# Attention outputs and output weights as float16 halves instead of fp32r halves

## The chip, the cores and the metric

The kernel runs on one core of one Trainium2 chip. The metric is the device time of one execution in microseconds. A profile of one execution lies beside the times; its engines are called PE (TensorE matmul), PEld (TensorE weight load), DVE (VectorE), ACT (ScalarE), POOL (GpSimd) and SP (SyncE, which issues the DMAs).

## The reference

A transformer block with adaptive layer norm: sliding-window attention over a cache, then a gated MLP. Cut to what matters:

```python
# x [1, 2048, 576]; k_cache, v_cache [1, 16, 2048, 128]; wq [576, 32*128]; wo [32*128, 576]
# w1, w3 [576, 4608]; w2 [4608, 576]; c [1, 576]; w_mod [576, 6*576]
sa, ca, ga, sb, cb, gb = split(silu(c) @ w_mod, 6)
h = layernorm(x) * (1 + ca) + sa
q = heads(h @ wq)                                   # 32 heads of 128
k, v = last 512 keys of the cache, each of 16 kv heads serving 2 query heads
p = softmax(q @ k.T * 128**-0.5)
x = x + ga * (concat_heads(p @ v) @ wo)
h = layernorm(x) * (1 + cb) + sb
out = x + gb * ((silu(h @ w1) * (h @ w3)) @ w2)     # everything in float32
```

## The kernel before

A float32 product is made from halves: each operand is split into a high part (the value rounded to a narrower type) and a low part (the rest), and three products are added: high times high, high times low, low times high. Most operands are split into two fp32r halves, which are 4 bytes each. The softmax weights `p` and the values `v` are already split into two float16 halves, scaled first so that float16 can hold them.

The 2048 rows are four blocks of 512. The attention phase walks 128 *slots*: first blocks 0 and 1 for all 32 heads (half 0), then blocks 2 and 3 for all heads (half 1). Mostly a head's two blocks are neighbouring slots, so in half 0 a new head begins at every even slot. Each slot has four *steps* (`t` = 0 to 3) of 128 query rows. The main loop (`for i in range(n + 2)`) writes the instructions of one step in a fixed order, and each engine runs its own in that order:

- the scores of this step (three products `pss`, then the row maximum `nm` on DVE), the transposes of an earlier step's `p` on PE (`turn_by_pe`, three steps behind), two to four products of the query projection for a later slot (`quad`);
- `weights`: the low half of an earlier transposed `p` (`turn`, on DVE), then the exponential on ACT;
- `attend_out`, nine steps behind: one head's output for 128 rows times the head's output weights. `back` makes six products of 128x288 (three pairs of halves, two halves of the 576 columns) into the PSUM tile `E`; DVE then multiplies `E` by `r`, one over the softmax sum, and adds it to the accumulator `acc`. There is one `E`, so the next step's `back` cannot begin before DVE has read it;
- `run(i, t)`: a table of side tasks put at fixed steps with `at(i, t, task, ...)`: loads, splits, and pieces that prepare the MLP's weights, which `lay` spreads over the steps by a table of POOL costs (`cost`).

At the end of a slot `values` makes `po`, the head's output, with twelve float16 products. ACT scales it into the high half `oth`, DVE makes the low half `otl`, and DVE takes the reciprocal `r`.

The output weights of a head (`wo`, 128x576) pass through half 0 once: `load_out` reads them, `gate` multiplies them by the gate on POOL, `split_out` writes the high half on ACT and the low half on POOL, and `store` writes both to DRAM (`kept`). In half 1 `reload` reads the halves back. `undo` undoes the per-row scale that `prepare_v` gave to `v`; before, ACT and DVE apply it as they read `po`.

After the attention phase (from about 1752 us in the profile) comes the MLP, which is PE work from end to end and does not use these functions.

Of the kernel before, what the change touches and what calls it, by code (L numbers as in the profile page):

```python
# [8 lines left out]
F32 = mybir.dt.float32  # L9
F32R = mybir.dt.float32r  # L10
F16 = mybir.dt.float16
AF = mybir.ActivationFunctionType
ALU = mybir.AluOpType
AX = mybir.AxisListType
# [3 lines left out]
P = 128  # L18
D = 576
# [3 lines left out]
SB = 512  # L23
NSB = S // SB
ST = SB // P
HQ, HKV, DH = 32, 16, 128
# [4 lines left out]
HALF = D // 2  # L31
# [11 lines left out]
ORDERED = {mybir.EngineType.PE, mybir.EngineType.DVE, mybir.EngineType.Activation, mybir.EngineType.Pool, mybir.EngineType.SP}  # L43
SCALE = float(DH) ** -0.5
LIFT = 2.0**14
BY_DMA = (0,)
AFTER_EXP = 3
SETTLE = 2
TINY = 1e-30
# [3 lines left out]
def tile_block(  # L53
# [16 lines left out]
    nc = tc.nc  # L70
    k0 = k_cache.shape[3] - W

    const = ctx.enter_context(tc.tile_pool(name="const", bufs=1))

    columns = ctx.enter_context(tc.tile_pool(name="columns", bufs=2))
# [20 lines left out]
    def half_split(a):  # L96
        return a.rearrange("p (a n) -> p a n", a=2)

    soon, then, running = [], [], []

    def do(jobs):
        due = jobs[:]
        jobs.clear()
        for job in due:
            job()
# [6 lines left out]
    def split_slowly(hi, lo, src, eng):  # L112

        if not running:
            return split(hi, lo, src, eng)
        nc.scalar.copy(hi, src)
        soon.append(lambda: eng.tensor_sub(lo, src, hi.bitcast(F32)))
# [108 lines left out]
    def norm_stats(b, t):  # L226
        if t == 0:
            norms[b] = odd.tile([P, ST, 2], F32, tag="mv", name="mv"), []
        st = odd.tile([P, 2, 6], F32, tag="bst", name="bst")
        for h in range(2):  # L230
            nc.vector.bn_stats(st[:, h, :], row(b, t)[:, h * HALF : (h + 1) * HALF])
        passing.pop((b, t), None)
        nc.vector.bn_aggr(norms[b][0][:, t, :], st.rearrange("p a b -> p (a b)"))
# [77 lines left out]
    kept = {}  # L311

    def store(h):
        kept[h] = dram.tile([P, 2, D], F32, name=f"kept{h}")
        for e, a in enumerate(wos[0, h]):
            nc.sync.dma_start(kept[h][:, e, :], a.bitcast(F32))

    def reload(h):
        o = pool.tile([P, 2, D], F32R, tag="o", name="o", bufs=3)
        nc.sync.dma_start(o.bitcast(F32), kept[h])  # L320
        return o[:, 0, :], o[:, 1, :]

    def load_in(w, lo):
# [14 lines left out]
        nc.sync.dma_start(raw, w[lo : lo + P, :])  # L338
        return raw

    def split_out(raw):
        o = pool.tile([P, 2, D], F32R, tag="o", name="o", bufs=3)
        split_slowly(o[:, 0, :], o[:, 1, :], raw, nc.gpsimd)
        return o[:, 0, :], o[:, 1, :]

    undo = const.tile([P, HKV], F32, name="undo")
    vkept = {}

    def turned_by_dma(out, pieces):
# [3 lines left out]
    def prepare_v(g, raw):  # L353

        vs = pool.tile([P, 2, W], F16, tag="kv", name="vs", bufs=8)
        u = columns.tile([P, 2], F32, tag="u", name="u", bufs=2)
        nc.vector.tensor_reduce(u[:, :1], raw, axis=AX.X, op=ALU.max, apply_absolute_value=True)
        nc.vector.tensor_scalar(u[:, :1], u[:, :1], TINY, 1.0 / LIFT, op0=ALU.max, op1=ALU.mult)
        nc.vector.reciprocal(u[:, 1:], u[:, :1])
        nc.vector.tensor_scalar(undo[:, g : g + 1], u[:, :1], 1.0 / LIFT, None, op0=ALU.mult)  # L360
        vals[0, g] = raw, u, vs

    def split_v(g):
# [159 lines left out]
    def values(i):  # L523
        half, h, b = slots[i]
        st = state[i]
        v, pt = vals[half, h // 2], st["pt"]
        po = bank("S", "po")
        steps = [(e, 0, j) for j in range(KC) for e in range(2)] + [(0, 1, j) for j in range(KC)]
        for k, (d, e, j) in enumerate(steps):
            nc.tensor.matmul(po, v[:, d, j, :], pt[:, e, j, :], start=k == 0, stop=k == 3 * KC - 1)  # L530
        oh = pool.tile([P, SB], F32R, tag="ah", name="oth", bufs=3)
        ol = pool.tile([P, SB], F32R, tag="al", name="otl", bufs=3)
        scale = undo[:, h // 2 : h // 2 + 1]
        nc.scalar.activation(oh, po, AF.Copy, scale=scale)  # L534
        nc.vector.scalar_tensor_tensor(ol, po, scale, oh.bitcast(F32), op0=ALU.mult, op1=ALU.subtract)  # L535
        r = columns.tile([P, ST], F32, tag="r", name="r", bufs=3)
        nc.vector.reciprocal(r, st["l"])
        st["o"], st["r"] = (oh, ol), r

    def attend_out(i, t):  # L540
# [478 lines left out]
    def at(i, t, task, *args):  # L1019

        tasks.setdefault((i, t), []).append((task, args))
# [33 lines left out]
    for key, i in first.items():  # L1055
        h, kv = key[1], (key[0], key[1] // 2)
        if 2 < i < 4 * PLAIN:
            at(i - 3, 1, load, wqs, key, load_in, wq1, h * DH)
            at(i - 2, 1, put, wqs, key, split_in)
        if key[0]:  # L1060
            at(i - 1, 0, load, wos, key, reload, h)
        elif i > 2:
            at(i - 2, 1, load, wos, key, load_out, wo, h * DH)
            at(*(i - 1, 0) if i > 6 else (i, 0), gate, wos, key, "a")
            at(*(i - 1, 2) if i > 6 else (i, 2), put, wos, key, split_out)
            at(i + 1, 0, store, h)
        if i > 2 and h % 2 == 0:
            at(i - 3, 0, load, keys, kv, load_k, h // 2)
            at(i - 2, 2, put, keys, kv, split_k)
            if key[0]:  # L1070
                at(i, 1, load, vals, kv, reload_v, h // 2)
            else:
                at(i - 2, 0, load_v, h // 2)
                put_v_at(4 * i - 3, h // 2)
                at(i + 1, 1, keep_v, h // 2)
# [7 lines left out]
    at(4, 1, keep_v, 1)  # L1083
    for h in range(3):
        at(*((0, 1), (1, 1), (2, 1))[h], load, wos, (0, h), load_out, wo, h * DH)
        at(*((1, 2), (2, 0), (3, 1))[h], gate, wos, (0, h), "a")
        at(*((1, 3), (2, 2), (3, 2))[h], put, wos, (0, h), split_out)
        at(3 + h, 0, store, h)

    last_group = len(groups) - 1  # L1090

# [72 lines left out]
    def lay(items, first, STEP):  # L1164

        spare = []

        def cost(task, args):
            if task is put:
                return {split_in: 1580, split_out: 1440}.get(args[2], 0)  # L1170
            return {gate: 1440, last_q: 1300, lower_v: 1300, norm_rows: 330, make_h: 1300}.get(task, 0)

        def pass_fixed(upto):
            while clock[0] < upto:
                fixed = sum(cost(*job) for job in tasks.get(divmod(clock[0], 4), ()))
                clock[1] = max(clock[1], clock[0] * STEP) + fixed
                clock[0] += 1

        clock = [first - 4, 0]
        step, ends = first, []  # L1180
        for number, (fill, pieces) in enumerate(items):
            begin = ends[number - 2] + 1 if number > 1 else first - LEAD + number
            at(*divmod(begin, 4), fill)
            step, when = max(step, begin + LEAD), []
            for (behind, ahead, after), jobs in pieces:
                if behind is not None:
                    step = max(step, when[behind] + 2)
                pass_fixed(step + 1)
                while clock[1] + ahead + after > (step + 1) * STEP + ROOM:
                    step += 1  # L1190
                    pass_fixed(step + 1)
                clock[1] += ahead + after
                when.append(step)
                work(step, *jobs)
            ends.append(step + 2)
        return step
# [264 lines left out]
    for i in range(n + 2):  # L1461
        run(i, -1)
        for t in range(ST):
            do(soon)
            if i <= n:
                halve(4 * i + t)
            if i == n:
                turn_by_pe(4 * i + t)
                turn(4 * i + t)
            if i < n:  # L1470
                made = scores(i, t)
                turn_by_pe(4 * i + t)
            if i + 1 < 4 * PLAIN:
                query(i + 1, t)
            for piece in qsteps.pop(4 * i + t, ()):
                quad(*piece)
            if i < n:
                weights(i, t, *made)
            do(then)
            if i >= m0:  # L1480
                for _ in range(3 if (i, t) == (n + 1, 0) else 1):
                    next(stream)
            for back_step in range(max(4 * i + t - 9, 0), 4 * i + t - 8 + ((i, t) == (n + 1, 3))):
                attend_out(*divmod(back_step, 4))
            run(i, t)
        if 1 <= i <= n:
            values(i - 1)
        if i == n:
            turning.close()
            after = ctx.enter_context(tc.tile_pool(name="after", bufs=1, space=PSUM))  # L1490
            lane[1] = (E, after.tile([P, 2, 512], F32, tag="T2", name="pf"))
# [65 lines left out]
```

## Time and profile before

| | |
|---|---|
| time, median of 3 runs | 2955.62 us (2955.44 to 2955.67) |
| profiled execution | 2954.41 us |
| its span in the profile | 2952.6 us |
| busy share of the span | PE 98%, PEld 81%, DVE 68%, ACT 53%, POOL 59% |
| granted TensorE clock | 0.998 |
| attention phase | up to about 1752 us, then the MLP |

The profiled execution is 1.2 us below the median, 0.04%. Products overlap in the PE's pipeline, so the duration of one product is longer than its share of the time; the distance from one start to the next is what a row of products costs. PEld shows weight loads, which run beside products.

### The profile page before, as it was taken

Reading aid. Unit: us, or ns where it says so; the run is one execution under the profiler, and the core shown is the slowest. Engines: PE = TensorE matmul, PEld = TensorE weight load, DVE = VectorE, ACT = ScalarE, POOL = GpSimd, SP = SyncE. Lnnn points to the kernel's source line nnn. Section 1 sums busy time; section 2 is a strip of 40 time slices with the busy share of each in tenths; the row PEclk is TensorE's granted clock in tenths of the full one; section 3 lists DMA queues with packets and bytes.
Section 4 is the critical chain, followed back from the end, with each engine's and each line's share of the span. In section 5 each row is a group of like instructions: output and inputs, shape, how many; then the busy total and the mean of one; then the engine's idle time right before and its main releaser. Section 6 shows DMA issues by size and latency. Waiting matters only on the chain.

```text
span 2952.6 us, 47355 instructions
## 1 busy us (share of the span) xinstructions
PE 2903.8 (98%) x16056; PEld 2384.8 (81%) x16056; DVE 2011.1 (68%) x3149; ACT 1560.9 (53%) x3251; POOL 1751.2 (59%) x1884
## 2 busy tenths in 40 slices
PE   7999999999999999999999999999999999999999
PEld 6777777777777777777777778888888888888887
DVE  7877787777777877777777766555555555555556
ACT  6667777777656776677677543333333222222322
POOL 3678888888712877777878223355564544334345
PEclk9999999999999999999999999999999999999999
DMA  6989999999885999989889946677766766666664
GB/s 216 280 266 347 277 345 311 298 289 299 260 277 179 326 301 295 296 284 283 273 278 299 300 154 202 218 233 251 251 226 202 286 231 199 205 198 193 202 201 143
DMA packets 441205, 751.27 MB, mean 254 GB/s; under 512 B 185730, under 2 KB 185730, under 8 KB 437380
## 3 DMA queue, kind: packets, MB, share of 16 engines
q1 hardware_dynamic: 440964, 748.25, 79.1%
q8 instruction: 128, 2.10, 0.3%
q14 instruction: 113, 0.93, 0.1%
HBM read 474.97 MB, written 235.37 MB: 241 GB/s over the span
## 4 chain that ended last, share of the span: by engine, by line
PE 80%; DVE 7%; ACT 4%; issue 2%; POOL 1%; DMA 1%; SPq 0%; ACTq 0%; POOLq 0%; DVEq 0%
PE py L797 15%; PE px L797 11%; PE po L530 10%; PE pe L428 10%; PE pf L910 7%; PE pe L910 7%; PE qy L797 5%; PE pt L505 4%; PE qx L797 3%; PE pss L466 2%; PE pss L468 2%; PE pss L467 2%; DVE nm L470 1%; DVE pt L515 1%; DVE acc L547 1%
## 5 line engine op out<-in xcount | busy, mean ns | idle before, releaser
L797 PE MATMUL py<-hset,wset 128*128 128x512 f32 x2016 | 507.2, 391 | 0.0
L547 DVE SCALAR_TENSOR_TENSOR acc<-pe,r,acc 128x576 f32<-128x576 f32 x510 | 413.6, 811 | 58.1 <-PE pe L428 55.4
L797 PEld LDWEIGHTS py<-hset,wset 128*128 128x128 f32 x2016 | 362.4, 188 | 59.0 <-ACT u L998 0.2
L428 PEld LDWEIGHTS pe<-o,oth 128*128 128x128 f32 x2040 | 319.7, 188 | 79.4 <-DVE acc L547 41.6
L797 PE MATMUL px<-hset,wset 128*128 128x512 f32 x1512 | 380.5, 391 | 0.0
L428 PE MATMUL pe<-o,oth 128*128 128x288 f32 x2040 | 360.1, 298 | 12.9 <-DVE acc L547 11.8
L530 PE MATMUL po<-pt,v 128*128 128x512 f16 x1536 | 353.8, 380 | 0.3 <-DMA v<-vs 0.3
L470 DVE TENSOR_REDUCE nm<-pss 128x1 f32<-128x512 f32 x512 | 345.6, 675 | 7.3 <-PE pss L468 7.1
L479 ACT ACTIVATE p<-pss,nm 128x512 f32<-128x512 f32 x384 | 265.7, 692 | 144.7 <-DVE nm L470 141.5
L697 POOL TENSOR_TENSOR wmade<-wraw,wmade 128x256 fp32r<-128x256 f32 x364 | 272.8, 749 | 115.5 <-issue 49.5
L110 POOL TENSOR_TENSOR akv<-u,akv 128x512 fp32r<-128x512 f32 x141 | 182.7, 1307 | 228.8 <-ACT akv L109 227.9
L797 PEld LDWEIGHTS px<-hset,wset 128*128 128x128 f32 x1512 | 275.5, 188 | 49.4
L509 ACT ACTIVATE pt<-pt 128x512 f16<-128x512 f32 x384 | 229.7, 598 | 136.6 <-PE pt L505 134.9
L535 DVE SCALAR_TENSOR_TENSOR otl<-po,undo,oth 128x512 fp32r<-128x512 f32 x128 | 96.1, 751 | 278.7 <-ACT oth L534 272.9
L515 DVE SCALAR_TENSOR_TENSOR pt<-pt 128x512 f16<-128x512 f32 x384 | 261.7, 681 | 28.7 <-ACT pt L509 28.3
L530 PEld LDWEIGHTS <-v 128*128 128x128 f16 x1536 | 140.6, 98 | 160.3 <-DMA v<-vs 0.6
L505 PEld LDWEIGHTS pt<-ident,p 128*128 128x128 f32 x1536 | 186.0, 140 | 72.0 <-PE pss L468 15.7
L505 PE MATMUL pt<-ident,p 128*128 128x128 f32 x1536 | 231.2, 273 | 9.4 <-DVE pt L515 6.4
L797 PE MATMUL qy<-hset,wset 128*128 128x512 f32 x784 | 237.0, 413 | 0.0
L466 PE MATMUL pss<-kh,qh 128*128 128x512 f32 x512 | 227.2, 444 | 6.3 <-ACT qh L109 2.2
L428 PE MATMUL pe<-o,otl 128*128 128x288 f32 x1020 | 217.5, 294 | 0.0
L468 PE MATMUL pss<-kh,ql 128*128 128x512 f32 x512 | 201.3, 393 | 0.9 <-DVE ql L110 0.9
(250 smaller groups left out, 5974.9 us busy)
## 6 DMA issues: line engine op xcount, KB each, us to landing
oset<-od SPq DMA_DIRECT2D x106, 576.0 KB, 4.7
od<-omade SPq DMA_DIRECT2D x133, 288.0 KB, 4.1
wraw<-in_B_w SPq DMA_DIRECT2D x36, 768.0 KB, 6.4
kept<-o SPq DMA_DIRECT2D x64, 288.0 KB, 5.1
o<-kept SPq DMA_DIRECT2D x32, 576.0 KB, 5.8
wraw<-in_A_wq_pairs SPq DMA_DIRECT2D x16, 768.0 KB, 6.3
w2raw<-in_B_w SPq DMA_DIRECT2D x38, 288.0 KB, 4.3
oset<-od SPq DMA_DIRECT2D x35, 288.0 KB, 3.2
```

The source lines that it names most:

```text
L428: nc.tensor.matmul(ps[:, h, :HALF], a[:, rows], b[:, h * HALF : (h + 1) * HALF], start=n == 0, stop=n == 2)
L466: nc.tensor.matmul(pss, st["qh"][:, rows], kh, start=True, stop=False)
L468: nc.tensor.matmul(pss, st["ql"][:, rows], kh, start=False, stop=True)
L470: nc.vector.tensor_reduce(nm, pss, axis=AX.X, op=ALU.max, negate=True)
L479: nc.scalar.activation(p, pss, AF.Exp, bias=nm, accum_out=st["l"][:, t : t + 1])
L505: nc.tensor.transpose(ps[:, j * P : (j + 1) * P], p[:, j * P : (j + 1) * P], ident)
L515: nc.vector.scalar_tensor_tensor(lo, p, LIFT, hi, op0=ALU.mult, op1=ALU.subtract)
L530: nc.tensor.matmul(po, v[:, d, j, :], pt[:, e, j, :], start=k == 0, stop=k == 3 * KC - 1)
L547: nc.vector.scalar_tensor_tensor(a, ps[:, :, :HALF], st["r"][:, t : t + 1], a, op0=ALU.mult, op1=ALU.add)
L697: nc.gpsimd.tensor_sub(t[:, 3:, :], x[:, :2, :], t[:, :2, :].bitcast(F32))
L797: nc.tensor.matmul(ps, w[:, a, :], h[:, b, :], start=start and n == 0, stop=n == 6, skip_group_check=True)
L910: nc.tensor.matmul(ps[:, h, :HALF], a[:, rows], w[:, b, :], start=m == 0, stop=m == 2)
```

## The change

The head's output and the output weights are split into float16 halves. To keep them inside float16's range, `po` is multiplied by a constant (`O_SCALE`), and the gated output weights by a factor per row. That factor comes from `undo` and a bound for the head: each row's largest magnitude times `undo` (`size_out`, DVE), summed over the 128 rows by a product with a matrix of ones into a spare column of `E` (`sum_out`, PE), and turned into factors (`scale_out`, four short DVE instructions). `even_out` scales the weights in place (ACT), `split_out` writes the high half (ACT) and, one step later, the low half (POOL). The inverse factor `whole_of` of the head is multiplied into `r` (one short DVE instruction in `values`). The stored halves are half as large and go out in one DMA instead of two. The tasks stand at other steps, `sum_out` is called through a new list `before` just ahead of `attend_out`, the layer norm's scratch tile `bst` has one buffer instead of two, and `undo` has four columns that are used in turn.

```diff
@@ store, reload
-        kept[h] = dram.tile([P, 2, D], F32, name=f"kept{h}")
-        for e, a in enumerate(wos[0, h]):
-            nc.sync.dma_start(kept[h][:, e, :], a.bitcast(F32))
+        kept[h] = dram.tile([P, 2, D], F16, name=f"kept{h}")
+        nc.sync.dma_start(kept[h], wos.pop((0, h, "whole")))
...
-        o = pool.tile([P, 2, D], F32R, tag="o", name="o", bufs=3)
-        nc.sync.dma_start(o.bitcast(F32), kept[h])
+        o = pool.tile([P, 2, D], F16, tag="o", name="o", bufs=3)
+        nc.sync.dma_start(o, kept[h])
@@ new tasks in place of split_out(raw)
+    def size_out(h):
+        raw = wos[0, h]
+        u = columns.tile([P, 2], F32, tag="u", name="wu", bufs=2)
+        nc.vector.tensor_reduce(u[:, :1], raw, axis=AX.X, op=ALU.max, apply_absolute_value=True)
+        nc.vector.tensor_mul(u[:, :1], u[:, :1], undo_of(h // 2))
+        wos[0, h] = raw, u
+    def sum_out(h):
+        raw, u = wos[0, h]
+        nc.tensor.matmul(E[:, h % 2, HALF : HALF + 1], ones, u[:, :1], start=True, stop=True)
+    def scale_out(h):
+        raw, u = wos[0, h]
+        whole = whole_of[:, h : h + 1]
+        nc.vector.tensor_scalar(u[:, :1], E[:, h % 2, HALF : HALF + 1], TINY, 1.0 / LIFT, op0=ALU.max, op1=ALU.mult)
+        nc.vector.reciprocal(u[:, 1:], u[:, :1])
+        nc.vector.tensor_mul(u[:, 1:], u[:, 1:], undo_of(h // 2))
+        nc.vector.tensor_scalar(whole, u[:, :1], 1.0 / O_SCALE, None, op0=ALU.mult)
+    def even_out(h):
+        raw, u = wos[0, h]
+        nc.scalar.activation(raw, raw, AF.Copy, scale=u[:, 1:])
+    def split_out(h):
+        raw, u = wos[0, h]
+        o = pool.tile([P, 2, D], F16, tag="o", name="o", bufs=3)
+        nc.scalar.copy(o[:, 0, :], raw)
+        wos[0, h], wos[0, h, "whole"] = (o[:, 0, :], o[:, 1, :]), o
+        soon.append(lambda: nc.gpsimd.tensor_sub(o[:, 1, :], raw, o[:, 0, :]))
@@ values
-        oh = pool.tile([P, SB], F32R, tag="ah", name="oth", bufs=3)
-        ol = pool.tile([P, SB], F32R, tag="al", name="otl", bufs=3)
-        scale = undo[:, h // 2 : h // 2 + 1]
-        nc.scalar.activation(oh, po, AF.Copy, scale=scale)
-        nc.vector.scalar_tensor_tensor(ol, po, scale, oh.bitcast(F32), op0=ALU.mult, op1=ALU.subtract)
+        oh = pool.tile([P, SB], F16, tag="ah", name="oth", bufs=3)
+        ol = pool.tile([P, SB], F16, tag="al", name="otl", bufs=3)
+        nc.scalar.activation(oh, po, AF.Copy, scale=O_SCALE)
+        nc.vector.scalar_tensor_tensor(ol, po, O_SCALE, oh, op0=ALU.mult, op1=ALU.subtract)
         r = columns.tile([P, ST], F32, tag="r", name="r", bufs=3)
         nc.vector.reciprocal(r, st["l"])
+        nc.vector.tensor_scalar(r, r, whole_of[:, h : h + 1], None, op0=ALU.mult)
@@ the table of tasks, half 0
-            at(i - 2, 1, load, wos, key, load_out, wo, h * DH)
-            at(*(i - 1, 0) if i > 6 else (i, 0), gate, wos, key, "a")
-            at(*(i - 1, 2) if i > 6 else (i, 2), put, wos, key, split_out)
-            at(i + 1, 0, store, h)
+            g = 4 * (i - 1)
+            at(*divmod(g + 1, 4), load, wos, key, load_out, wo, h * DH)
+            at(*divmod(g + 3, 4), gate, wos, key, "a")
+            at(*divmod(g + 4, 4), size_out, h)
+            at(*divmod(g + 5, 4), before.append, lambda h=h: sum_out(h))
+            at(*divmod(g + 6, 4), scale_out, h)
+            at(*divmod(g + 7, 4), even_out, h)
+            at(*divmod(g + 8, 4), split_out, h)
+            at(i + 2, 0, store, h)
```

On PE, the last step of a slot: `back` and the first products of `values`. Before, a product of fp32r halves loads its own weights and the wait for `E` stands on the whole of it:

```order
L428 MATMUL pe<-o,oth 128x288 [waits DVE_49]
L428 MATMUL pe<-o,oth 128x288 x3
L428 MATMUL pe<-o,otl 128x288 x2
L530 LDWEIGHTS v [waits DMAHW0_49,DMAHW4_49]
L530 MATMUL po<-pt,v 128x512 [waits Activation_49]
```

Now, at the same place, the load is an instruction of its own:

```order
L463 LDWEIGHTS oth
L463 MATMUL pe<-o,oth 128x288 [waits DVE_49]
L463 LDWEIGHTS oth
L463 MATMUL pe<-o,oth 128x288
L463 LDWEIGHTS oth
L463 MATMUL pe<-o,oth 128x288
L463 LDWEIGHTS oth
L463 MATMUL pe<-o,oth 128x288
```

The wait for DVE moved from load and product together to the product alone.

On DVE, the first three steps of an even slot in half 0 (a slot in which a new head begins; `nm` is the row maximum, `pt` and `p` the low halves of softmax weights, `acc` the accumulation that frees `E`). Before:

```order
L470 TENSOR_REDUCE nm<-pss 128x1
L515 SCALAR_TENSOR_TENSOR pt<-pt 128x4x128
L547 SCALAR_TENSOR_TENSOR acc_579<-pe,r,acc_579 128x576
L470 TENSOR_REDUCE nm<-pss 128x1
L515 SCALAR_TENSOR_TENSOR p_7613<-pt,p_7613 128x512
L515 SCALAR_TENSOR_TENSOR pt<-pt 128x4x128
L547 SCALAR_TENSOR_TENSOR acc_560<-pe,r,acc_560 128x576
L470 TENSOR_REDUCE nm<-pss 128x1
L515 SCALAR_TENSOR_TENSOR pt<-pt 128x4x128
L547 SCALAR_TENSOR_TENSOR acc_560<-pe,r,acc_560 128x576
```

Now, from the first `acc` of the same slot to the second row of `scale_out`:

```order
L582 SCALAR_TENSOR_TENSOR acc_580<-pe,r,acc_580 128x576
L351 TENSOR_REDUCE wu<-oraw 128x1
L352 TENSOR_TENSOR wu<-wu,undo 128x1
L505 TENSOR_REDUCE nm<-pss 128x1
L550 SCALAR_TENSOR_TENSOR p_7850<-pt,p_7850 128x512
L550 SCALAR_TENSOR_TENSOR pt<-pt 128x4x128
L582 SCALAR_TENSOR_TENSOR acc_561<-pe,r,acc_561 128x576
L505 TENSOR_REDUCE nm<-pss 128x1
L550 SCALAR_TENSOR_TENSOR pt<-pt 128x4x128
L582 SCALAR_TENSOR_TENSOR acc_561<-pe,r,acc_561 128x576
L364 TENSOR_SCALAR wu<-pe 128x1
L365 RECIPROCAL wu<-wu 128x1
```

Seven DVE instructions are new in such a slot: the product with `whole_of` at its head (in every slot), the two of `size_out` behind the first `acc`, and the four of `scale_out` behind the third, where the next rows are its last two.

More of the change, by code (lines that the diff above doesn't have):

```diff
@@ L45 @@
 LIFT = 2.0**14
+O_SCALE = 2.0**-22
 BY_DMA = (0,)
@@ L97, in half_split @@
         return a.rearrange("p (a n) -> p a n", a=2)
-    soon, then, running = [], [], []
+    soon, then, before, running = [], [], [], []
     def do(jobs):
@@ L228, in norm_stats @@
             norms[b] = odd.tile([P, ST, 2], F32, tag="mv", name="mv"), []
-        st = odd.tile([P, 2, 6], F32, tag="bst", name="bst")
+        st = odd.tile([P, 2, 6], F32, tag="bst", name="bst", bufs=1)
         for h in range(2):
@@ L339, in load_out, with undo_of @@
         return raw
[L341 to L346, printed above, removed]
+    undo = const.tile([P, 4], F32, name="undo")
+    whole_of = const.tile([P, HQ], F32, name="whole_of")
+    def undo_of(g):
+        return undo[:, g % 4 : g % 4 + 1]
+    def size_out(h):
[23 more added lines that the diff above has]
+        soon.append(lambda: nc.gpsimd.tensor_sub(o[:, 1, :], raw, o[:, 0, :]))
     vkept = {}
@@ L359, in prepare_v @@
         nc.vector.reciprocal(u[:, 1:], u[:, :1])
-        nc.vector.tensor_scalar(undo[:, g : g + 1], u[:, :1], 1.0 / LIFT, None, op0=ALU.mult)
+        nc.vector.tensor_scalar(undo_of(g), u[:, :1], 1.0 / LIFT, None, op0=ALU.mult)
         vals[0, g] = raw, u, vs
@@ L1085, in tile_block @@
         at(*((0, 1), (1, 1), (2, 1))[h], load, wos, (0, h), load_out, wo, h * DH)
-        at(*((1, 2), (2, 0), (3, 1))[h], gate, wos, (0, h), "a")
-        at(*((1, 3), (2, 2), (3, 2))[h], put, wos, (0, h), split_out)
-        at(3 + h, 0, store, h)
+        at(*((1, 1), (2, 0), (3, 0))[h], gate, wos, (0, h), "a")
+        g = (6, 9, 13)[h]
+        at(*divmod(g, 4), size_out, h)
+        at(*divmod(g + 1, 4), sum_out, h)
+        at(*divmod(g + 1, 4), scale_out, h)
+        at(*divmod(g + 1, 4), even_out, h)
+        at(*divmod(g + 1, 4), split_out, h)
+        at(4 + h, 0, store, h)
     last_group = len(groups) - 1
@@ L1169, in cost @@
             if task is put:
-                return {split_in: 1580, split_out: 1440}.get(args[2], 0)
-            return {gate: 1440, last_q: 1300, lower_v: 1300, norm_rows: 330, make_h: 1300}.get(task, 0)
+                return {split_in: 1580}.get(args[2], 0)
+            return {gate: 1440, split_out: 1440, last_q: 1300, lower_v: 1300, norm_rows: 330, make_h: 1300}.get(task, 0)
         def pass_fixed(upto):
@@ L1482, in tile_block @@
                     next(stream)
+            do(before)
             for back_step in range(max(4 * i + t - 9, 0), 4 * i + t - 8 + ((i, t) == (n + 1, 3))):
```

## Prediction

> **What bounds the kernel now.** I read the engine lines of the page first, then busy time by stretch, then the waits, then PE's and DVE's timelines of one slot.
>
> ```profile
> PE 2903.8 (98%) x16056; PEld 2384.8 (81%) x16056; DVE 2011.1 (68%) x3149; ACT 1560.9 (53%) x3251; POOL 1751.2 (59%) x1884
> 74.00:910.00 836.00, 821.07 (x4591) 638.30 (x4590) 642.47 (x1082) 582.84 (x1267) 599.56 (x698) 1.00 0.92 291
> 910.00:1752.00 842.00, 831.74 (x4676) 649.61 (x4674) 632.89 (x1019) 569.80 (x1266) 565.14 (x714) 1.00 0.88 278
> 1752.00:2953.00 1201.00, 1192.03 (x6512) 1051.36 (x6510) 678.07 (x936) 361.60 (x631) 558.54 (x441) 1.00 0.66 215
> ```
>
> The last three rows are half 0, half 1 and the MLP, roughly: length, then busy PE, PEld, DVE, ACT, POOL, then clock and the DMA share. In both halves of attention PE is busy 98 to 99% of the time, DVE 75 to 77%, ACT and POOL about 70%. So PE's work sets the time, and all that is to be won from other engines is the 25 us in which PE is idle there (14.9 + 10.3). What makes PE wait:
>
> ```profile
> PEld pe L428 <- DVE acc L547: 41.6, 79, 1.2
> PE pe L428 <- DVE acc L547: 11.8, 28, 1.0
> ACT oth L534 <- PE po L530: 164.7, 118, 3.5
> ```
>
> The columns are total us, times, longest us. `back` waits 107 times (79 + 28) for DVE to have read `E`; with 128 slots that is nearly once a slot. The timelines of one even slot of half 0 (start us, us; what an engine waited for in brackets) show where, PE first:
>
> ```profile
> 603.07 0.69 PE L428 MATMUL pe<-o,oth 128*128 128x288 f32 x4
> 603.59 0.42 PE L428 MATMUL pe<-o,otl 128*128 128x288 f32 x2
> 603.86 0.40 PE L466 MATMUL pss<-kh,qh 128*128 128x512 f32 x1
> 604.09 0.39 PE L467 MATMUL pss<-kl,qh 128*128 128x512 f32 x1
> ...
> 607.92 0.79 PE L428 MATMUL pe<-o,oth 128*128 128x288 f32 x4
> 608.55 0.42 PE L428 MATMUL pe<-o,otl 128*128 128x288 f32 x2
> 608.82 2.77 PE L530 MATMUL po<-pt,v 128*128 128x512 f16 x12
> 611.23 0.58 PE L466 MATMUL pss<-kh,qh 128*128 128x512 f32 x1
> 611.65 0.39 PE L467 MATMUL pss<-kl,qh 128*128 128x512 f32 x1
> ```
>
> ```profile
> 599.98 0.75 DVE L535 SCALAR_TENSOR_TENSOR otl<-po,undo,oth 128x512 fp32r<-128x512 f32 x1 [2.51 <-ACT oth L534]
> 600.65 0.17 DVE L537 RECIPROCAL r<-l 128x4 f32<-128x4 f32 x1
> 600.73 0.66 DVE L470 TENSOR_REDUCE nm<-pss 128x1 f32<-128x512 f32 x1
> 606.45 0.69 DVE L515 SCALAR_TENSOR_TENSOR pt<-pt 128x512 f16<-128x512 f32 x1 [0.59 <-ACT pt L509]
> 607.05 0.81 DVE L547 SCALAR_TENSOR_TENSOR acc<-pe,r,acc 128x576 f32<-128x576 f32 x1
> ```
>
> DVE starts at `otl`, works nearly without a pause to the third `acc`, which ends at 607.86, and then has 2.5 us to wait while PE makes the twelve products of `values`. PE's `back` of the last step begins 0.06 us behind that `acc`. So a slot is bound by PE, but its first three steps are short enough that DVE is nearly the bound too.
>
> **The change, part by part.** The durations that it needs (ns, least/median/most):
>
> ```profile
> L534 ACT ACTIVATE oth<-po,undo x128: 672/689/695, 51.6 to 1737.7; 128x512 fp32r<-128x512 f32 x128
> L509 ACT ACTIVATE pt<-pt x384: 579/597/632, 39.0 to 1730.2; 128x512 f16<-128x512 f32 x192
> L535 DVE SCALAR_TENSOR_TENSOR otl<-po,undo,oth x128: 737/751/753, 52.3 to 1738.5; 128x512 fp32r<-128x512 f32 x128
> L515 DVE SCALAR_TENSOR_TENSOR pt<-pt x384: 658/680/694, 40.5 to 1731.2; 128x512 f16<-128x512 f32 x192
> L357 DVE TENSOR_REDUCE u<-kraw x15: 670/674/678, 54.8 to 827.8; 128x1 f32<-128x512 f32 x15
> L358 DVE TENSOR_SCALAR u<-u x16: 153/153/155, 28.2 to 828.5; 128x1 f32<-128x1 f32 x16
> L366 ACT ACTIVATE kraw<-kraw,u x15: 711/724/746, 59.6 to 830.7; 128x512 f32<-128x512 f32 x15
> L117 POOL TENSOR_TENSOR o<-oraw,o x32: 1407/1428/1893, 54.9 to 857.3; 128x576 fp32r<-128x576 f32 x32
> L372 POOL TENSOR_TENSOR vs<-kraw,vs x15: 1151/1162/1172, 63.8 to 832.3; 128x512 f16<-128x512 f32 x15
> L208 PE MATMUL ps_vec<-sc,wm x16: 169/250/271, 14.4 to 16.3; 128*128 128x1 f32 x16
> ```
>
> A. *The products themselves.* No row shows a float16 product of 288 columns, so I bound it. Six fp32r products of 288 columns take 603.07 to 603.86, 0.79 us, 132 ns each. At 512 columns fp32r takes 0.23 us (603.86 to 604.09) and float16 0.217 us: twelve of them and one fp32r product take 608.82 to 611.65. By columns, 288 of 512 of 217 ns is 122 ns, so a step's six would take 0.73 us and save 0.06. Against this the type changes twice more in each step. The change that the trace has, around `values`, costs no more than some 0.01 us each way (with both changes in it, the twelve still come to 217 ns each on average); I take 0.02 us a step. Net 0.04 us by 512 steps: **-20 us**; ends 0 (no gain in spacing) and -30 (changes free).
>
> B. *The load behind the wait.* Where `back` waited, its six products and their load took 607.92 to 608.82, 0.90 us, against 0.79 where it did not: 0.11 us for a load that stood behind the wait too. Now only the product waits. Over 107 waits -12 us, and 0 if the loads gain nothing; some waits end before the load would have been late, so **-8 us**.
>
> C. *What DVE keeps.* In a slot in which DVE's row sets the last `back`, the gain of the first three steps (3 x 0.04) only lengthens the wait. In others DVE itself waits for PE or ACT within the row, and a faster PE pulls it along. I take half of the 107 slots: **+6 us**; ends 0 and +13.
>
> D. *The start of DVE's row.* `oth` and `otl` now have constants and float16 results, like the rows of `pt`: 689 to 597 and 751 to 680 ns, 0.16 us less. The new product of `r` (128x4) is at most the reciprocal's 0.17. In the 53 slots of C this is between -8 and +1 us: **-2 us**.
>
> E. *Sizing a head, 32 times, half 0 only.* The reduction of 576 is 674 x 576/512 = 0.76 us, and five short instructions at 0.15 each: 1.5 us of DVE per head, 48 us in all if none of it is covered. The first two (0.9 us) stand behind the first `acc`; DVE's waits later in that row (0.59 at 606.45 in this slot) take most of it. The first row of `scale_out` stands between the third `acc` and the release of `E`, 0.15 us, bare. The last three fall before the 2.5 us in which DVE waits anyway. I take 0.3 us for the half of the heads whose slot already waits, 0.07 for the rest: **+6 us**; ends 0 and +48.
>
> F. *The product with ones.* The fp32 products with one column (16 records for eight products) stand within 2.0 us, so at most 0.25 us each, on PE: 32 x 0.25 = 8 us, +11 with a load behind the wait on `E`. Half falls into slots where PE then waits for DVE: **+4 us**; ends 0 and +11.
>
> G. *Heads 0 to 2* run all stages within two steps, where PE has no older work to hide the chain reduction, sum, scaling: about 1 us each, **+3 us**, ends 0 and +6.
>
> At nothing: the second ACT pass over the weights (724 x 576/512 = 0.81 us) stands in the last step ahead of `oth`, where ACT waits for `po` 118 times, 1.4 us on average; without that cover it would be up to 26 us. POOL's subtraction gets cheaper (1428 to about 1162 x 576/512 = 1307 ns), its `gate` is as before and is due a step before DVE needs it. The transfers shrink:
>
> ```profile
> kept<-o SPq DMA_DIRECT2D x64, 288.0 KB, 5.1
> o<-kept SPq DMA_DIRECT2D x32, 576.0 KB, 5.8
> ```
>
> 64 stores become 32 of the same size and the reloads halve, 18.9 MB less at a DMA share of 0.88 to 0.92; no wait of PE on these names them, so no gain is counted, and SP's queue has 32 issues fewer. `bst` with one buffer serialises instructions that run on DVE in order anyway.
>
> Sum: -20 - 8 + 6 - 2 + 6 + 4 + 3 = **-11 us**, 2943.4 for the profiled execution of 2954.4 us. The runs' median is 1.2 us above it, so 2944.6, I say **2945 us**.
>
> **The rivals.**
>
> *R1, DVE becomes the bound in half 0 (slower).* If the waits of 0.59 us move with the work, as they do where ACT waits for a row maximum that DVE now gives later, each head costs its slot the full 1.05 us of E ahead of the last `back`, 34 us in place of 6: +17, **about 2972**. It decides from 17 us for E, 0.53 us per head. For it: DVE has no other long pause in the row above. Against: that slot's 0.59.
>
> *R2, the waits swallow the gain (no change).* C at +13, E at +12: -11 + 7 + 6 = +2, **about 2958**. For it: 107 waits in 128 slots.
>
> *R3, the gain comes through.* Where DVE's row follows PE, C and E fall to 0 and A comes to -24: **about 2928**. Against it stands the same row of waits.
>
> *R4, the spacing is one of width, not of type,* so that float16 keeps 132 ns at 288 columns: A is 0 and the type changes cost 10: +19, **about 2975**. Against: 0.23 and 0.217 at the same width of 512. The Trainium skill's page TensorE: Matmul & The Clock Gate, section Back-to-back issue gap, has a rule of this kind: start to start is N/2.4 + 2.5 ns when warm, with no term for the type, which makes 122.5 ns of 288 columns for either; by it A would be 0. The trace agrees with it for float16 (216 at 512 columns) and not for fp32r (230 at 512 and 132 at 288), so the measurement decides.
>
> **How the numbers follow.** The sum and its near neighbourhood (2938 to 2951) have 0.47, R3 0.15, R2 0.18, R1 0.16, R4 0.04. The range reaches from below R3's value to short of R1's, 2925 to 2968; outside it lie a third of R3 and most of R1 and R4. About 0.2%, 6 us, is what a measurement of this kernel can tell from none. Faster: nearly all of the first two, 0.59. Same: R2 and the slow edge of the sum, 0.22. Slower: the rest, 0.19.
>
> **What the profile after would show.** A: six products of `back` in 0.74 to 0.76 us where they do not wait, loads near 98 ns. B: `back` after a wait is no longer than without. C: the wait of `pe` on `acc` stays once a slot and grows in half 1 by up to 0.1 us. E: in half 0 it grows in even slots, by 0.3 us or less; a growth of 1 us there is R1. F: a pair of one-column products of 0.25 us ahead of 32 `back`s. Half 1, which has neither E nor F, must gain more than half 0: I expect about -10 us there and about none in half 0. What would make the prediction wrong: side tasks that land on other steps (POOL's and ACT's pieces are spread by the cost table) and lengthen ACT's row before a `pt`, which in the slot above is what DVE waits for; and a `gate` on POOL that comes late for the reduction, which would hold up all of DVE behind it.

## Result, and the profile after

| | before | after |
|---|---|---|
| time, median | 2955.64 us (2955.44 to 2957.45) | 2996.35 us (2991.57 to 2997.78) |
| profiled execution | 2954.41 us | 2996.51 us |
| its span | 2952.6 us | 2994.7 us |

The change makes the kernel slower: the ratio is 1.0134, 95% interval [1.0116, 1.0151], or 41 us. The forecast was 2945 us, with a range of 2925 to 2968.

Where the time went is read first from busy time by stretch, with the stretches cut where the halves now end (length, then busy PE, PEld, DVE, ACT, POOL, clock, DMA share, GB/s):

```profile
74.00:949.00 875.00, 832.85 (x4666) 564.53 (x4665) 716.97 (x1327) 597.41 (x1301) 589.97 (x698) 1.00 0.86 266
949.00:1794.00 845.00, 824.36 (x4674) 565.19 (x4673) 650.78 (x1083) 564.69 (x1266) 561.83 (x714) 1.00 0.86 267
1794.00:2994.00 1200.00, 1192.12 (x6512) 1051.35 (x6510) 678.38 (x936) 361.43 (x631) 557.54 (x441) 1.00 0.65 215
```

The MLP is as long as before. In half 0, PE is now idle for 42 us (875.00 - 832.85) where it was 15, in half 1 for 21 us where it was 10. The clock is 1.00. So the loss is waiting, nearly all in attention. The start of the products `po` of each slot, set against the kernel before, gives the course of it: 8.8 us behind at slot 8, 38.7 at the end of half 0 (slot 64), 42.2 at the end of attention. Half 1 alone loses 3.6 us, where a gain was expected.

What PE waits for, first before and then after (us in all, times, longest):

```profile
PEld pt L505 <- DVE pt L515: 10.5, 47, 0.7
PE pt L505 <- DVE pt L515: 6.4, 28, 0.8
```

```profile
PEld pt L540 <- DVE pt L550: 42.6, 81, 1.7
PE pt L540 <- DVE pt L550: 28.7, 48, 1.6
PEld pt L540 <- DVE p L550: 18.5, 32, 1.3
PEld pe L358 <- DVE acc L582: 13.0, 27, 1.9
PE pe L463 <- DVE acc L582: 12.2, 27, 1.5
```

The wait that grew is not the one for `E`. It is the transposes' wait for DVE to have read the tile `pt` of the step before: DVE is late earlier in its row than at `acc`. DVE's own lines say why (busy us, mean ns):

```profile
L572 DVE TENSOR_SCALAR r<-r,whole_of 128x4 f32<-128x4 f32 x128 | 47.2, 369 | 4.5
L351 DVE TENSOR_REDUCE wu<-oraw 128x1 f32<-128x576 f32 x32 | 23.6, 738 | 0.0
L352 DVE TENSOR_TENSOR wu<-wu,undo 128x1 f32<-128x1 f32 x32 | 10.0, 313 | 1.1
L366 DVE TENSOR_TENSOR wu<-wu,undo 128x1 f32<-128x1 f32 x32 | 11.7, 365 | 1.1
```

The smallest new instruction, a product of 128x4, is the dearest: 47.2 us. The slot that the prediction showed, as it runs now, DVE and then POOL (start us, us):

```profile
627.35 0.69 DVE L569 SCALAR_TENSOR_TENSOR otl<-po,oth 128x512 f16<-128x512 f32 x1 [2.28 <-ACT oth L568]
627.96 0.17 DVE L571 RECIPROCAL r<-l 128x4 f32<-128x4 f32 x1
628.16 1.03 DVE L572 TENSOR_SCALAR r<-r,whole_of 128x4 f32<-128x4 f32 x1
629.11 0.68 DVE L505 TENSOR_REDUCE nm<-pss 128x1 f32<-128x512 f32 x1
629.71 0.68 DVE L550 SCALAR_TENSOR_TENSOR pt<-pt 128x512 f16<-128x512 f32 x1
```

```profile
627.88 1.28 POOL L1172 TENSOR_TENSOR hc<-hc 128x512 f32<-128x512 f32 x1
```

```profile
630.44 0.66 PE L540 MATMUL pt<-ident,p 128*128 128x128 f32 x4 [0.70 <-DVE pt L550]
```

POOL's instruction runs from 627.88 to 629.16. DVE's product is issued during it, at 628.16, and ends at 629.19, just behind it. The row maximum `nm` starts at 629.11, 1.15 us after the reciprocal; before, it started 0.08 us after it (600.65 to 600.73). Two rows on, PE stands for 0.70 us. In all 128 slots the product took 228 ns at least; in 57 it took more than 240, and the 49 above 300 end 23 to 28 ns after an instruction of POOL. Of the 84 products that start while POOL runs, 54 are among these 57; for the other 30, POOL had at most 0.22 us left. Of the 64 rows `wu<-wu,undo`, 30 took more than 240 ns, and they end 14 to 19 ns after an instruction of POOL. The page SBUF — State Buffer of the Trainium skill, section Who interferes with whom, has a rule for this: a DVE `tensor_scalar` from SBUF to SBUF that can use two ports shares a port pair with GpSimd as an exclusive lock, and whichever comes second waits for the whole instruction of the other; a DVE instruction with two inputs in SBUF is held likewise while GpSimd reads SBUF. The product of `r` is of the first kind, the two rows `wu<-wu,undo` of the second, and the trace agrees with both.

But the lock is not the larger part. Summed over the slots, from the start of the reciprocal to the start of the next work that is not on `r`, DVE took 11.0 us before and 61.9 after. Of the 50.9 us more, what lies above 229 ns in the product is 17.9 us. The rest, some 33 us, is there without any lock: 0.26 us a slot. The experiments take the two apart.

### The profile page after: what moved, and what is told of

It is laid out like the page before. It is cut to its first block, busy times and chain, and to the rows that moved or that the text cites. A ratio compares the mean times of both kernels' runs of the same rounds, so it can differ in the third digit from the quotient of the medians.

```text
span 2994.7 us, 47581 instructions
## 1 busy us (share of the span) xinstructions
PE 2906.4 (97%) x16120; PEld 2223.7 (74%) x16120; DVE 2104.4 (70%) x3469; ACT 1570.3 (52%) x3283; POOL 1737.1 (58%) x1884
## 4 chain that ended last, share of the span: by engine, by line
PE 72%; DVE 15%; ACT 6%; issue 3%; POOL 2%; DMA 2%; SPq 0%; POOLq 0%; ACTq 0%; DVEq 0%
PE py L832 15%; PE px L832 11%; PE po L565 8%; PE pe L463 8%; PE pf L945 7%; PE pe L945 6%; PE qy L832 4%; PE pt L540 3%; DVE nm L505 3%; DVE acc L582 2%; PE qx L832 2%; DVE pt L550 2%; PE pss L501 2%; PE pss L503 2%; PE pss L502 2%
## 5 line engine op out<-in xcount | busy, mean ns | idle before, releaser
L463 PE MATMUL pe<-o,oth 128*128 128x288 f16 x2040 | 337.9, 288 | 14.3 <-DVE acc L582 12.2
L463 PEld LDWEIGHTS <-oth 128*128 128x128 f16 x2048 | 167.2, 99 | 175.1 <-issue 131.9
L501 PE MATMUL pss<-kh,qh 128*128 128x512 f32 x512 | 261.4, 511 | 14.0 <-ACT pt L514 5.6
L565 PEld LDWEIGHTS <-v 128*128 128x128 f16 x1536 | 150.3, 98 | 157.2
L569 DVE SCALAR_TENSOR_TENSOR otl<-po,oth 128x512 f16<-128x512 f32 x128 | 88.4, 690 | 250.9 <-ACT oth L568 248.4
L463 PE MATMUL pe<-o,otl 128*128 128x288 f16 x1020 | 208.5, 286 | 0.0
L502 PE MATMUL pss<-kl,qh 128*128 128x512 f32 x512 | 202.5, 396 | 0.0
```

The costliest lines, as they stand in the source:

```text
L463: nc.tensor.matmul(ps[:, h, :HALF], a[:, rows], b[:, h * HALF : (h + 1) * HALF], start=n == 0, stop=n == 2)
L501: nc.tensor.matmul(pss, st["qh"][:, rows], kh, start=True, stop=False)
L502: nc.tensor.matmul(pss, st["qh"][:, rows], kl, start=False, stop=False)
```

## Experiments

Each time is set against runs of the kernel before that were taken beside it: 2955.84 us for e1 to e4, 2956.54 for e5 to e8, 2957.58 for e9 to e12. The difference to it is what is compared; for the changed kernel it is +40.7 us.

The theory (T1) was that DVE is held by POOL at the product of `r`, and so starts its row late in every slot; its rivals were the sizing of a head in half 0 (T2), tasks moved to other steps (T3), and float16 halves that gain nothing (T4). T5, that the dependence on the reciprocal is most of the price, came after e5 to e8.

### Parts of the change left out

```diff
 e1_no_r_product: the product with whole_of is left out
-        nc.vector.tensor_scalar(r, r, whole_of[:, h : h + 1], None, op0=ALU.mult)
```

> Left out: the product of r by whole_of in values, so the heads' outputs keep a factor. 128 DVE instructions of 128x4 are gone, nothing else. T1 (that product is held until a running POOL instruction ends, and DVE's row of every slot starts late by it): 51 us of DVE go from the start of r to the next DVE instruction, and the time falls by 25 to 45 us, to 2950 to 2972, more in half 0 than in half 1. T2 (the sizing of a head on DVE in half 0 is the whole cause): at 128 times 60 ns, at most 8 us fall, to 2988 or more. T3 (side tasks now stand at other steps and make ACT, POOL or a DMA late): no change, 2990 to 2998. T4 (float16 halves gain nothing on PE): says nothing of this run.

Measured: 2954.01 us, ratio 0.9995 [0.9985, 1.0004], -1.8 us against before and -42.5 against the changed kernel. T2 and T3 fall as sole causes.

```diff
 e2_no_sizing: whole_of is one, the weights are scaled by one
+    nc.gpsimd.memset(whole_of, 1.0)
...
-        nc.scalar.activation(raw, raw, AF.Copy, scale=u[:, 1:])
+        nc.scalar.activation(raw, raw, AF.Copy, scale=ones[:, :1])
...
-            at(*divmod(g + 4, 4), size_out, h)
-            at(*divmod(g + 5, 4), before.append, lambda h=h: sum_out(h))
-            at(*divmod(g + 6, 4), scale_out, h)
... (heads 0 to 2)
-        at(*divmod(g, 4), size_out, h)
-        at(*divmod(g + 1, 4), sum_out, h)
-        at(*divmod(g + 1, 4), scale_out, h)
```

> Left out: the bound of a head (size_out, sum_out, scale_out); the weights are scaled by one and whole_of is one everywhere, the product of r stays. T1 alone (the product of r, 0.4 us a slot, is all): the time falls by no more than 10 us, to 2986 or more, and half 1 does not change. T2 (sizing alone): it falls by 30 to 45 us, to 2951 to 2966, all of it in half 0. Both causes together, which I hold likeliest: it falls by 20 to 35 us, to 2961 to 2976, all in half 0, and half 1 stays 4 us slower than in the kernel before. T3: no change.

Measured: 2970.18 us, ratio 1.0051 [1.0036, 1.0066], +14.3 us against before. Attention is 10.5 us behind at slot 64 and loses 3.8 more in half 1, as the changed kernel does: the product of `r` acts in both halves, the sizing in half 0 only.

```diff
 e3_types_only: both edits above
```

> Left out: both the bound of a head and the product of r, so that the float16 types, the second pass over the weights, the split and the moved tasks are what is left of the change. T1 and T2 together: 2925 to 2942, faster than the kernel before by 13 to 30 us, in both halves alike (the 38 ns a step of the products, 512 times, less what the waits take). T3: 2975 to 2995, still slower than before. T4: about the time of the kernel before, 2950 to 2960.

Measured: 2936.26 us, ratio 0.9937 [0.9922, 0.9952], -19.6 us. So the float16 halves do gain, and T4 falls. Half 0 gains 4.3 us and half 1 14.6, not both alike as expected.

```profile
L464 PEld LDWEIGHTS <-oth 128*128 128x128 f16 x2048 | 164.4, 98 | 182.4 <-issue 137.8 <-ACT p L531 7.7 <-ACT pt L545 5.5
PE pe L464 <- DVE acc L582: 13.4, 27, 1.2
PE pt L541 <- DVE pt L551: 3.3, 7, 1.0
```

The waits of the products for `pt` are smaller than in the kernel before (3.3 us against 6.4). The products of `back` wait for `acc` as often as before (27 times here, 28 there). The three kernels are a table of two parts: with neither -19.6, with the product alone (e2) +14.3, with the sizing alone (e1) -1.8, with both +40.7. The product alone adds 33.9 us, the sizing alone 17.8, both together 60.3: 8.6 more than their sum.

### The same work at another place

```diff
 e4_r_early, in values: r and its product stand ahead of oth and otl
+        nc.vector.reciprocal(r, st["l"])
+        nc.vector.tensor_scalar(r, r, whole_of[:, h : h + 1], None, op0=ALU.mult)
...
         nc.scalar.activation(oh, po, AF.Copy, scale=O_SCALE)
         nc.vector.scalar_tensor_tensor(ol, po, O_SCALE, oh, op0=ALU.mult, op1=ALU.subtract)
-        nc.vector.reciprocal(r, st["l"])
-        nc.vector.tensor_scalar(r, r, whole_of[:, h : h + 1], None, op0=ALU.mult)
```

> Nothing is left out: the reciprocal r and its product are written ahead of oth and otl, so that DVE runs them in the 2.5 us in which it waits for the products of values, and not at the head of its next row. T1: the product is held as long as before, mean 0.37 us and up to 1.1, but DVE waits there anyway; the time falls as without the product, by 25 to 45 us, to 2950 to 2972, and the waits of PE for pt shrink with it. T2 and T3: no change beyond 8 us.

Measured: 2955.74 us, ratio 1.0001 [0.9992, 1.0011], -40.8 us against the changed kernel, with every instruction of it kept. The line of the product:

```profile
L568 DVE TENSOR_SCALAR r<-r,whole_of 128x4 f32<-128x4 f32 x128 | 60.3, 471 | 4.5
```

It is held longer than in the changed kernel (471 ns on average, 369 there), and that costs nothing, since DVE waits there for the products of `values` anyway. What this instruction costs is set by what stands behind it.

### Lock or dependence

```diff
 e5_r_by_columns: four products of one column at the same place
-        nc.vector.tensor_scalar(r, r, whole_of[:, h : h + 1], None, op0=ALU.mult)
+        for t in range(ST):
+            nc.vector.tensor_scalar(r[:, t : t + 1], r[:, t : t + 1], whole_of[:, h : h + 1], None, op0=ALU.mult)
```

> Nothing is left out: at the same place as in the changed kernel, the product of r by whole_of is made as four products of one column (128x1) in place of one of 128x4. T1 (the 128x4 form takes the port that POOL holds, the one-column form, like that of whole_of itself with its 139 to 149 ns, does not): none of the 512 products takes over 160 ns, DVE's next instruction starts 0.4 to 0.8 us after r does, always the same, where it was 0.34 to 1.1; the time falls by 0 to 20 us, to 2976 to 2996, since four instructions cost as much as the lock did on average. If the delay comes from anything that holds the queue and not from the form (a wait for whole_of, a semaphore), the first of the four is long as often as now, mean over 300 ns, and the time rises.

Measured: 3023.05 us, ratio 1.0222 [1.0208, 1.0236], +66.5 us. The time was missed, and so was the length (160 ns at most), but the form is not held:

```profile
L573 DVE TENSOR_SCALAR r<-r,whole_of 128x1 f32<-128x1 f32 x512 | 73.8, 207 | 4.5
```

All 512 take 201 to 216 ns, so this form is never held, though 200 of them start with over 250 ns of an instruction of POOL still to run. But the next instruction now starts 0.70 us after the reciprocal in every slot (0.693 to 0.701), 89.1 us in all: more than with the lock. It was this run that showed that an unlocked short instruction is not cheap either.

```diff
 e7_before_plus_r_product: the kernel BEFORE, one line more
         nc.vector.reciprocal(r, st["l"])
+        nc.vector.tensor_scalar(r, r, ones[:, :1], None, op0=ALU.mult)
```

> The kernel before, with one instruction more: a product of r (128x4) by a column of ones, behind the reciprocal in values, as the change has it. T1: the product is held by POOL as in the changed kernel, 228 to 1100 ns, mean 0.37, and the time rises by 15 to 40 us, to 2970 to 2995, in half 0 and half 1 alike (DVE's row is nearly the bound in both). Rival (the product only hurts because the changed kernel has more on DVE's row, or other neighbours): a rise of under 8 us.

Measured: 3001.70 us, ratio 1.0155 [1.0139, 1.0170], +45.2 us, above the range that T1 gave; half 0 loses 24.9 us and half 1 20.9. This one line, in the kernel before, costs as much as the whole change.

```profile
L538 DVE TENSOR_SCALAR r<-r,ones 128x4 f32<-128x4 f32 x128 | 50.5, 394 | 4.5
PEld pt L505 <- DVE pt L515: 51.4, 89, 2.2
```

The same wait of PE as in the changed kernel appears, with nothing else changed. DVE's way from `r` to the next instruction grows by 54.0 us (65.0 against 11.0), and the time by 45.2: 0.84 of it.

```diff
 e10_before_plus_one_column: the kernel BEFORE, a product of one column of r
+        nc.vector.tensor_scalar(r[:, :1], r[:, :1], ones[:, :1], None, op0=ALU.mult)
```

> The kernel before, with one instruction more in values: the first column of r is multiplied by a column of ones (128x1), which does not change it. The form was never held in e5_r_by_columns, but the instruction waits for the reciprocal ahead of it. T5 (most of the price of the product of r is that a short dependent instruction stands between two long ones, and the lock by POOL only adds to it): 0.2 to 0.25 us a slot from r to the next instruction on top of 0.084, none over 0.4 in all, and the time rises by 24 to 32 us, to 2980 to 2988. T1 alone (the lock is the price): a rise of at most 10 us.

```diff
 e11_before_plus_apart: the kernel BEFORE, a product that doesn't depend on r
-        r = columns.tile([P, ST], F32, tag="r", name="r", bufs=3)
-        nc.vector.reciprocal(r, st["l"])
+        r = columns.tile([P, ST + 1], F32, tag="r", name="r", bufs=3)
+        nc.vector.reciprocal(r[:, :ST], st["l"])
+        nc.vector.tensor_scalar(r[:, ST:], ones[:, :1], ones[:, :1], None, op0=ALU.mult)
```

> The kernel before, with one instruction more at the same place that does not depend on the reciprocal: a column of ones by a column of ones into a spare fifth column of r. T5: without the dependence it costs 0.06 to 0.13 us a slot, and the time rises by 7 to 16 us, to 2963 to 2972. If dependence does not matter, it costs as much as in e10_before_plus_one_column.

Measured: e10 2983.66 us, ratio 1.0085 [1.0070, 1.0100], +26.1 us; e11 2967.16 us, ratio 1.0031 [1.0020, 1.0042], +9.6 us. DVE's timeline of one slot, e10 first:

```profile
606.52 0.17 DVE L537 RECIPROCAL r<-l 128x4 f32<-128x4 f32 x1
606.72 0.21 DVE L538 TENSOR_SCALAR r<-r,ones 128x1 f32<-128x1 f32 x1
606.85 0.68 DVE L470 TENSOR_REDUCE nm<-pss 128x1 f32<-128x512 f32 x1
```

```profile
604.11 0.17 DVE L537 RECIPROCAL r<-l 128x4 f32<-128x4 f32 x1
604.19 0.18 DVE L538 TENSOR_SCALAR r<-ones 128x1 f32<-128x1 f32 x1
604.29 0.68 DVE L470 TENSOR_REDUCE nm<-pss 128x1 f32<-128x512 f32 x1
```

In e11 the instructions overlap: 84 ns from the reciprocal to the product, 0.10 from it to `nm`. In e10 the product has to see the reciprocal finished (it waits on DVE's own semaphore, which the one in e11 doesn't) and starts only 0.20 us after it. So the price of the product of `r` splits in three: an instruction more, +9.6 us; its dependence on the one ahead, +16.5 (26.1 - 9.6); the 128x4 form, which POOL can hold, +19.1 (45.2 - 26.1). In that last step the row grows by 22.3 us, and 21.2 of them lie above 229 ns in the product, so it is nearly all lock. T5 holds; T1 names the smaller half. The Trainium skill's page VectorE: DVE Perf Modes, section The DRAIN you can't avoid, says that chaining DVE instructions without semaphores saves nothing, and measures eight copies at the same time with and without. For short instructions these two runs say otherwise, and they decide here.

```diff
 e12_before_r_early: the kernel BEFORE, r ahead of oth and otl, as in e4
+        r = columns.tile([P, ST], F32, tag="r", name="r", bufs=3)
+        nc.vector.reciprocal(r, st["l"])
...
-        r = columns.tile([P, ST], F32, tag="r", name="r", bufs=3)
-        nc.vector.reciprocal(r, st["l"])
```

> The kernel before, with the reciprocal r written ahead of oth and otl and nothing else: DVE then makes it in its pause. If DVE's row passes its time on nearly one to one, as the 45 us of e7_before_plus_r_product for some 47 us on the row say, the 11 us that the reciprocal holds up the row (128 times 84 ns) are gained: 2945 to 2950. If only half the slots are bound by DVE's row (the prediction's 107 waits in 512 steps): 2949 to 2953; if none: 2955.

Measured: 2954.18 us, ratio 0.9988 [0.9979, 0.9996], -3.4 us against before, with an interval of -1 to -6 us; the profiled execution has attention end only 0.2 us earlier, but its slot 0 starts 2.2 us late, so that 2.4 us are gained from there on. As a difference, -3.4 us fits the second of the three expectations (half the slots) best, and not the first. Taking 11 us off DVE's row gains about a third of them (0.1 to 0.6 by the interval). With e11 (12.7 us more on the row, +9.6), e10 (31.7, +26.1) and e7 (54.0 over all 128 slots, where the expectation has some 47; +45.2) the share that passes to the time is 0.3, 0.75, 0.82, 0.84. Within their intervals the last three are alike; e12 lies clear of e10 and e7. So of time added to DVE's row most comes through, and of time taken off it less.

### A better version

```diff
 e6_all_in_shadow: e4, and in half 0 the sizing at other steps
-            at(*divmod(g + 1, 4), load, wos, key, load_out, wo, h * DH)
-            at(*divmod(g + 3, 4), gate, wos, key, "a")
-            at(*divmod(g + 4, 4), size_out, h)
-            at(*divmod(g + 5, 4), before.append, lambda h=h: sum_out(h))
-            at(*divmod(g + 6, 4), scale_out, h)
+            at(*divmod(g, 4), load, wos, key, load_out, wo, h * DH)
+            at(*divmod(g + 2, 4), gate, wos, key, "a")
+            at(*divmod(g + 3, 4), size_out, h)
+            at(*divmod(g + 4, 4), before.append, lambda h=h: sum_out(h))
+            at(*divmod(g + 7, 4), scale_out, h)
```

> Nothing is left out: r and its product stand ahead of oth and otl as in e4_r_early, and in half 0 the sizing of a head moves by a step or so: loads and gate a step earlier, size_out at the last step of a slot, the sum one step later, scale_out at the last step of the slot with the head. Theory: of the 20 us by which e4_r_early is slower than e3_types_only nearly all is DVE work of the sizing that stands ahead of the last back of a slot, so in the 2.5 us of DVE's pause it costs little: 2933 to 2945, faster than both kernels. Rival (the sizing costs PE the products with ones and the waits on E, 32 times 0.3 to 0.6, wherever DVE does it): 2948 to 2956.

Measured: 2950.72 us, ratio 0.9978 [0.9969, 0.9987], -5.8 us. Of the two, the rival's range holds it: the place is worth some 6 us, not most of the 20.

```diff
 e8_r_early_one_column: e4, and a scalar column in place of a second tensor, in size_out and scale_out
-        nc.vector.tensor_mul(u[:, :1], u[:, :1], undo_of(h // 2))
+        nc.vector.tensor_scalar(u[:, :1], u[:, :1], undo_of(h // 2), None, op0=ALU.mult)
-        nc.vector.tensor_mul(u[:, 1:], u[:, 1:], undo_of(h // 2))
+        nc.vector.tensor_scalar(u[:, 1:], u[:, 1:], undo_of(h // 2), None, op0=ALU.mult)
```

> Nothing is left out: e4_r_early, and the two products by undo in size_out and scale_out are written as products with a scalar column in place of two tensors (128x1 each). T1: the form with two inputs in SBUF is held by POOL too (158 to 1028 and 159 to 1487 ns there, 21.5 us in all for 64), the form with a scalar column is not: 139 to 160 ns each, 9.6 us in all, and the time falls by 3 to 10 us against e4_r_early, to 2946 to 2953. If length does not follow the form, both stay as they are and so does the time.

Measured: 2949.94 us, ratio 0.9977 [0.9967, 0.9987], -6.6 us. The 64 products take 212 to 216 ns each (13.7 us for all, 21.5 in e4): longer than expected, but never held. Length follows the form, as T1 said.

```diff
 e9_shadow_one_column: e6 and e8, and for heads 1 and 2
-        at(*divmod(g + 1, 4), sum_out, h)
+        if h:
+            at(*divmod(g, 4), before.append, lambda h=h: sum_out(h))
+        else:
+            at(*divmod(g + 1, 4), sum_out, h)
```

> Nothing is left out: the moves of e6_all_in_shadow and the one-column products of e8_r_early_one_column together, and for heads 1 and 2 the product with ones is issued ahead of the next step's attend_out (through the list before) and not behind the last one. If the two add (each gained 5 to 6 us on e4_r_early) and the first slots, which lie 9 to 11 us behind the kernel before in both, lose 2 to 3 us less: 2940 to 2946. If they gain the same time twice (the pause of DVE is worth only so much): 2947 to 2951.

Measured: 2943.81 us, ratio 0.9954 [0.9942, 0.9967], -13.8 us, as expected if the gains add. It is faster than both kernels. That the gains of e6 and e8 add in full isn't shown: at slot 8 it is 4.7 us behind the kernel before, e6 8.7 and e8 10.9, so 4 to 6 us may be owed to heads 1 and 2, which were not tried alone. It is 3.8 us behind at slot 64 and gains 15.0 in half 1.

```profile
PEld pt L540 <- DVE pt L550: 10.7, 21, 0.7
PE pe L463 <- DVE acc L582: 10.5, 22, 1.2
PE pt L540 <- DVE pt L550: 3.8, 12, 0.9
```

PE's waits for `pt` are back where they were before the change, with the new work still on DVE.

## Why the prediction was wrong, step by step

**The step that failed is D,** "the start of DVE's row", taken at -2 us. It set 0.16 us saved in `oth` and `otl` against a product of "at most the reciprocal's 0.17", and counted both in the 53 slots of C only. Two things in it were wrong.
- *The price.* The reciprocal costs the row 84 ns because the next instruction overlaps it. A product that depends on it starts only 0.20 us behind it and adds 0.26 us unheld; with the lock it is 0.40 on average (50.9 us over 128). The duration of an instruction in a row was taken for its price; the starts of its neighbours would have given it. Nor did the prediction ask which of DVE's new instructions POOL can hold.
- *The share of slots.* C's half of the slots describes the kernel before: there, shortening DVE's row by 11 us gave about a third of it (e12). But of a price in every slot more comes through: 0.75 of 0.10 us a slot (e11) and 0.84 of 0.42 (e7). The share read from the waits of before was too small for work added, even for little of it.

In place of -2, the product of `r` cost 34 us without the sizing and 42.5 with it.

**E** (+6, ends 0 and +48) was mis-sized: without the product of `r`, all of the sizing with F and G costs 17.8 us (e1 against e3), where +13 stood for the three; with it, 26.4. DVE's part is 59.9 us, 1.87 per head and not 1.5, because the two products with two tensors take 313 and 365 ns on average in place of 150. F's products with ones begin behind waits for `acc` (13.0 us, 27 times), which is part of this.

**A and B** hold, and so does the wait that C rests on. From the start of the products before a step's `back` to those after it, the six took 1255 ns with their neighbours before and 1217 after, 38 ns a step, where the working had 40. Their loads are 98 ns, as said. The prediction's count of 107 waits took 79 of a load and 28 of a product together, and the two mostly stand in one step: counting idle times over 60 ns, 36 steps have both and 66 the load's alone. By starts, the first product of `back` comes over 300 ns behind the product ahead of it in 67 steps before, 71 in e3 and 74 after, where 234 to 239 ns is usual. So this wait did stay, in somewhat more than half of the slots. In the 54 steps ahead of `values` that follow on `qy`, the median from the products before `back` to those after it falls from 1467 to 1303 ns in e3, and the shortest, which has no wait, from 1241 to 1191: the 0.11 us more is what B said. All that is left without the product and the sizing gives -19.6 us; A to C together gave -22, and D without the product would have been -8 at most. Half 1 gains 14 to 15 us as soon as `r` is out of the way (e1, e3, e4), more than the 10 expected.

**G** (+3): at slot 8 the changed kernel is 8.8 us behind, e3 without any sizing 4.9; counted from the start of slot 0, which varies by some 2 us between the profiles, it is 8.3 and 2.8. So 4 to 5.5 us are G (e1, without the product of `r`, is 9.3 behind at slot 8), and 3 to 5 come from what the sum had at nothing: the second ACT pass, the split and the moved tasks in slots where DVE also makes the modulation rows. Which of them it is was not tried, and stays open.

**The rivals.** R1 had the right engine and the right sign, but its place, the sizing in half 0, is the smaller part: alone it gives 2954 (e1). What the types do by themselves (2936, e3) lies between R3's 2928 and the forecast, R2 did not occur, and R4 falls: at 288 columns float16 products follow each other at 122 ns and fp32r at 132, so the gain of A is real. What was named as able to make the prediction wrong, moved tasks and a late `gate`, did not: moved tasks have at most a part in the 3 to 5 us above, and `size_out` never waits for `gate` (0.0 in its row above).

## What to carry to other kernels

A small instruction at the head of the row of an engine that is nearly the bound is priced by the start of the next one, not by its own duration: add the dependence on the instruction ahead of it, ask whether another engine can hold its form, and reckon with most of the tiles, not only with those that wait today. Before writing it there, look for that engine's pause in the same slot: the same two lines, a few lines earlier, made 41 us. Try the new instruction alone in the old kernel; here that one line lost 45 us, as much as the whole change.

## What the runs showed of the hardware that was not expected

- On DVE, a short instruction that waits for the reciprocal ahead (169 ns) starts 0.20 us after it, one that doesn't 0.08 us (e10 and e11).
- A one-column product with a scalar column takes 179 to 216 ns (e5, e8, e10, e11), with constants 139 to 149 (`whole_of` in the changed kernel). Neither was held by POOL in any of these; 128x4 products and those with two tensors in SBUF were, up to 1.5 us (1473 ns in e8, 1487 in e4).
- In e8, PE waits 1.6 us for `acc` ahead of a product with ones at 65 us, and behind it the granted clock falls for some 4 us; products of 512 columns that stand 0.23 us apart elsewhere stand 0.42 us apart there:

```profile
66.00:70.00 4.00, 4.00 (x14) 2.37 (x14) 1.85 (x6) 2.71 (x5) 2.06 (x2) 0.58 1.10 255
```

e1, e4 and e6 have the same wait and show the same (0.64, 0.62 and 0.61); the changed kernel has the wait and keeps 1.00. By the row it is worth some 1.7 us (0.42 of the 4); what decides it was not tried.
